# A second buffer for the split queries and keys, and two prepared weights fewer ahead of the first MLP

## The chip, the core and the metric

The kernel runs on one core of a Trainium2 chip. The time is that of the device in microseconds (us) for one execution, and the median of several executions stands for a kernel. The engines of a core are TensorE (PE; the loads of its stationary operand are listed apart as PEld), VectorE (DVE), ScalarE (ACT), GpSimd (POOL) and SyncE (SP), which here issues nearly all DMAs. Each engine takes its instructions strictly in the order in which they were written for it.

## The reference

```python
# B, H, S, D = 4, 8, 576, 64; all float32 (some MLP weights come as float64)
q_rot, k_rot = rotate(q), rotate(k)                       # rotary embedding over D
scores = D ** -0.5 * q_rot @ k_rot.T                      # per batch and head: 576 x 576
attn = softmax(scores)
x = (attn @ v) as [2304 tokens, 512]                      # heads side by side
g = s * relu(x @ w_in) ** 2 + b                           # first MLP: 512 -> 2048
x = g @ w_out                                             # 2048 -> 512
out = (silu(x @ w_gate) * (x @ w_val)) @ w_out2           # second MLP: 512 -> 1536 -> 512
```

## The kernel before

Float32 accuracy is kept by splitting every matmul operand into a high part (rounded to the format that PE multiplies) and a low part (the rest); a product is then two or three matmuls, high by high and the mixed ones.

**Attention** goes over 16 pairs of heads. For each pair, `prep(p)` loads q and k into a tile `x` (two buffers), rotates them on POOL in four steps that end at L495, and transposes them on PE (`pst`, L515) in three groups. From each group ACT writes the high part into the tile `qkhi` (L524) and DVE the low part into `qklo` (L526). Ten DMAs from SP (L548) then copy pieces of `qkhi` and `qklo` to other partitions, into the operand tiles `a`, `t` and `kz`. Of these there are two sets, one for even and one for odd pairs, so the copies of pair p wait until the scores of pair p-2 are done. `pair(p)` computes nine strips of scores (`ps_s`, L620), their maximum on DVE (L623) and exponentials on ACT (L627, tile `e`), transposes those (`ps_t`, L681), splits them into `ph` (ACT, L689) and `pl` (DVE, L696) and multiplies by v (`ps_av`).

`qkhi` and `qklo` have one buffer each. So L524 of pair p, which writes the first group, has to wait until the last copy of pair p-1 has landed.

**First MLP**, in blocks of 512 tokens (later ones 384): for each of 16 chunks f of 128 hidden features, 12 matmuls give `hb` (L810 to L812) from the block's tokens `xh`, `xl` and the split weight "in f"; ACT and DVE make `gh` and `gl` (DVE L872); 12 matmuls with "out f" add to `acc`. PE runs hb of chunk f+2 after acc of chunk f. A weight is loaded as raw float64 (`raw`, three buffers), turned into float32 by one ACT and three DVE instructions (L304, L307, L310, L315, tile `dec`, two buffers), and split by ACT (L342) and by POOL or DVE (L349, tile `w`). The order of the 32 weights is in 0, out 0, in 1, out 1, and so on. The first `WA = 10` of them have memory outside of what attention uses and are prepared while attention runs, the z-th not before a certain strip of scores, their L349 on POOL. The other 22 go into a pool that takes attention's memory when it is free (`switch`, `sw`), so their loads wait for the end of attention, and their L349 is on DVE. The tokens of the first block come from DRAM during attention (`x_load`: loads, a sum and a scaling with `rbx` on POOL at L790 and L793, a split on ACT L797 and DVE L799).

**The order** of all instructions is not written by hand. Each step is given to `Schedule` as an operation with an engine, a duration, a priority (lower goes first), the operations that it needs, and tokens for the buffers that it takes and frees. `Schedule.run` plays this through with its own assumed durations, and whenever an engine is free it emits the ready operation of best priority. The instruction order on every engine is what comes out of this; on the chip each engine keeps that order, whatever the real durations are.

Of the kernel before, what the change touches and what calls it, by code (L numbers as in the profile page):

```python
# [9 lines left out]
F32R = mybir.dt.float32r  # L10
# [167 lines left out]
def tile_attention_moe_moe(  # L178
# [17 lines left out]
    B, H, S, D = q.shape  # L196
# [8 lines left out]
    NU = PC  # L205
    QA = PC // 2
    UBS = (512, 512, 512, 384, 384)
    WA = 10
    WB = 22
    NE = 7  # L210
    LATE, LAST = 1 << 20, 1 << 21
    WARM = 75
    TP = 100
# [8 lines left out]
    sch = Schedule()  # L222
    op = sch.op
    sch.free.update({
        "raw": 3, "dec": 2, "wa": WA, "x": 2, "vr": 2, "ry": 1, "hi": 1, "vh": 3, "opb0": 1, "opb1": 1, "l": 2, "lb": 2, "cr": 1, "e": NE, "ph": 2, "pl": 2,
        "xr": 2, "rbx": 1, "s": 2, "t": 3, "v": 1, "xhb": 1, "gb": 2, "rb2": 3,
    })

# [1 line left out]
    dram = ctx.enter_context(tc.tile_pool(name="dram", bufs=1, space=DRAM))  # L230
    wa_p = ctx.enter_context(tc.tile_pool(name="wa", bufs=WA))
    raw_p = ctx.enter_context(tc.tile_pool(name="raw", bufs=3))
    dec_p = ctx.enter_context(tc.tile_pool(name="dec", bufs=2))
    late = {}
# [11 lines left out]
    att = ExitStack()  # L246
# [2 lines left out]
    vr_p = att.enter_context(tc.tile_pool(name="vr", bufs=2))  # L249
    rp_p = att.enter_context(tc.tile_pool(name="rp", bufs=1))  # L250
    v_p = att.enter_context(tc.tile_pool(name="v", bufs=3))
    ph_p = att.enter_context(tc.tile_pool(name="ph", bufs=2))
    pl_p = att.enter_context(tc.tile_pool(name="pl", bufs=2))
    e_p = att.enter_context(tc.tile_pool(name="e", bufs=NE))
# [169 lines left out]
    def prep(p):  # L424
# [6 lines left out]
        st = {} if p else first_st  # L431
# [30 lines left out]
        for g in range(G):  # L462
            cs = slice(g * PC // G, (g + 1) * PC // G)
            eng = "dve" if p == 0 else "pool"
            e = nc.vector if eng == "dve" else nc.gpsimd
            tt = t_dve if eng == "dve" else t_pool
            wide = [128, PC // G, 2, D // 2]
            def views(a, cs=cs):
                return st["x"].rearrange("p c j (a d) -> p c j a d", a=2)[:, cs, :, a], st["ry"][:, cs, :, a]
            def r0(g=g, e=e, views=views, cs=cs, wide=wide):  # L470
                if g == 0:
                    st["ry"] = rp_p.tile([128, PC, 2, 2, D // 2], F32, tag="ry", name="ry")
                e.tensor_tensor(out=views(0)[1], in0=views(1)[0], in1=rt[:, cs, 1:2].to_broadcast(wide), op=ALU.mult)
            def r1(e=e, views=views, cs=cs, wide=wide):
                e.tensor_tensor(out=views(1)[1], in0=views(0)[0], in1=rt[:, cs, 1:2].to_broadcast(wide), op=ALU.mult)
            def r2(e=e, cs=cs):
                xv = st["x"].rearrange("p c j (a d) -> p c (j a) d", a=2)[:, cs]
                e.tensor_tensor(out=xv, in0=xv, in1=rt[:, cs, 0:1].to_broadcast([128, PC // G, 4, D // 2]), op=ALU.mult)
            def r3(e=e, views=views):
                e.tensor_tensor(out=views(0)[0], in0=views(0)[0], in1=views(0)[1], op=ALU.subtract)  # L480
            def r4(e=e, views=views):
                e.tensor_tensor(out=views(1)[0], in0=views(1)[0], in1=views(1)[1], op=ALU.add)
            o = st.get("rope")
            if o is None and p:
                def y0():
                    st["ry"] = rp_p.tile([128, PC, 2, 2, D // 2], F32, tag="ry", name="ry")
                    nc.gpsimd.tensor_tensor(out=views2(0)[1], in0=views2(1)[0], in1=rt[:, :, 2:3].to_broadcast(whole), op=ALU.mult)
                def y1():
                    nc.gpsimd.tensor_tensor(out=views2(1)[1], in0=views2(0)[0], in1=rt[:, :, 1:2].to_broadcast(whole), op=ALU.mult)
                def y2():  # L490
                    xv = st["x"].rearrange("p c j (a d) -> p c (j a) d", a=2)
                    nc.gpsimd.tensor_tensor(out=xv, in0=xv, in1=rt[:, :, 0:1].to_broadcast([128, PC, 4, D // 2]), op=ALU.mult)
                def y3():
                    xv = st["x"].rearrange("p c j d -> p (c j d)")
                    nc.gpsimd.tensor_tensor(out=xv, in0=xv, in1=st["ry"].rearrange("p c j a d -> p (c j a d)"), op=ALU.add)  # L495
                n2 = PC * D
                for y, fn in enumerate((y0, y1, y2, y3)):
                    o = op("pool", t_pool(n2 if y < 2 else 2 * n2), fn, pr, (o, *lds[0], *rt_op), (ry_tok,) if y == 0 else (), (ry_tok,) if y == 3 else ())
                st["rope"] = o
            elif not p:  # L500
              o = None
              for y, fn in enumerate((r0, r1, r2, r3, r4)):
                deps = [o, *lds[g], rt_op[g]]
                if y == 0 and g > 0:
                    deps.append(st["first"])
                o = op(eng, tt(fd if y == 2 else fd // 2), fn, pr + g, deps, (ry_tok,) if y == 0 and g == 0 else (),
                       (ry_tok,) if y == 4 else (), port=eng == "dve")
                if y == 0 and g == 0:
                    st["first"] = o
            ps_tok = Token("t")  # L510
            def tr(g=g):
                st["ps", g] = ps = ps_t.tile([128, 512], F32, tag="t", name="pst")
                rv = st["x"].rearrange("p c j d -> p c (j d)")
                for c in range(PC // G):
                    nc.tensor.transpose(taken(ps)[:, :, c * 64:(c + 1) * 64], rv[:, g * (PC // G) + c], ident.rearrange("p (h r) -> p h r", h=2))  # L515
            acq = (ps_tok, hi_tok if p > 1 else tok) if g == 0 else (ps_tok,)
            prt = pr + 3 + g
            o = st["tr"] = op("pe", 0.33, tr, prt, (o, eye_op, st.get("tr"), *(zeros[z] if p < 2 else ())), acq, (x_tok,))
            if p > 1:
                def hi(g=g):  # L520
                    if g == 0:
                        st["hi"] = rp_p.tile([128, 2 * S], F32R, tag="hi", name="qkhi")
                        st["lo"] = rp_p.tile([128, 2 * S], F32R, tag="lo", name="qklo")
                    nc.scalar.activation(out=place(st["hi"], g), in_=taken(st["ps", g]), func=AF.Copy, scale=qs_t)  # L524
                def lo(g=g):
                    nc.vector.scalar_tensor_tensor(  # L526
                        out=place(st["lo"], g), in0=taken(st["ps", g]), scalar=qs_t, in1=place(st["hi"], g).bitcast(F32), op0=ALU.mult, op1=ALU.subtract
                    )
                o = st["hi0"] = op("act", t_act(CG, True, 1), hi, prt, (o, qs_op, st.get("hi0")))
                trs.append(op("dve", t_dve(CG, 2), lo, prt, (o,), (), (ps_tok,)))  # L530
            else:
                def act(dst, rows, g=g):
                    scale = D ** -0.5 if rows is up else 1.0
                    return lambda: nc.scalar.activation(out=place(dst, g), in_=taken(st["ps", g])[rows], func=AF.Copy, scale=scale)
                def sub(dst, src, rows, g=g):
                    scale = D ** -0.5 if rows is up else 1.0
                    return lambda: nc.vector.scalar_tensor_tensor(
                        out=place(dst, g), in0=taken(st["ps", g])[rows], scalar=scale, in1=place(src, g).bitcast(F32), op0=ALU.mult, op1=ALU.subtract
                    )
                o1 = op("act", t_act(CG), act(t[dn], dn), prt, (o,))  # L540
                o2 = op("act", t_act(CG), act(a[up], up), prt, (o,))
                ops += [o1, o2, op("dve", t_dve(CG), sub(a[dn], a[up], up), prt, (o2,), (), (ps_tok,))]
                ops.append(op("act", t_act(CG), act(kz[up], dn), prt, (o,), (), (ps_tok,)))
                ops.append(op("dve", t_dve(CG), sub(t[up], t[dn], dn), prt, (o1,), (), (ps_tok,)))
# [373 lines left out]
    n_att = len(sch.ops)  # L918
    for z in range(WA):
        weight(("out" if z % 2 else "in", z // 2), ("wa",), TP * NP, after=s_turns[WU0 + WUS * z:][:1])  # L920
# [8 lines left out]
    def block_b(i, j):  # L929
        st = {}  # L930
        UB = UBS[j]
        prio = LATE + 1000 * i
        pieces, deps, batches = [], [], []
        for o, m, b, s in x_pieces(sum(UBS[:j]), UB, S):
            pieces.append((o, m, (x_d[0][b][:, s:s + m], x_d[1][b][:, s:s + m])))
            batches.append((b, s, m, o))
            deps += x_store[b]
        outs, xh_tok = x_load(st, pieces, UB, prio - 800 if i else LATE - 900, deps, ("xhb", "xhc"), lambda: late[st["xh_tok"].pool], batches, "dve" if i else "pool")
        toks = (Token("s"), Token("s"))

        def get_acc(m):
# [430 lines left out]
```

## Time and profile before

| | |
|---|---|
| time, median of 3 (range) | 1137.23 us (1137.05 to 1138.14) |
| profiled execution: time, span | 1137.79 us, 1136.0 us |
| PE busy, PEld busy | 1106.9 us (97%), 1010.6 us (89%) |
| DVE, ACT, POOL busy | 799.5 us (70%), 591.2 us (52%), 191.0 us (17%) |
| mean granted TensorE clock | 0.991 |

Shares are over the whole span, and its stages differ. Attention lasts until about 317 us and keeps four engines busy; the first MLP's first block follows until about 403 us. After that PE is busy in practically every slice, and the page shows DVE and ACT far from full there. The ends of matmuls are modelled, so short pauses between them don't show as idle time.

### The profile page before, as it was taken

Reading aid. Unit: us, or ns where it says so; the run is one execution under the profiler, and the core shown is the slowest. Engines: PE = TensorE matmul, PEld = TensorE weight load, DVE = VectorE, ACT = ScalarE, POOL = GpSimd, SP = SyncE. Lnnn points to the kernel's source line nnn. Section 1 sums busy time; section 2 is a strip of 40 time slices with the busy share of each in tenths; the row PEclk is TensorE's granted clock in tenths of the full one; section 3 lists DMA queues with packets and bytes.
Section 4 is the critical chain, followed back from the end, with each engine's and each line's share of the span. In section 5 each row is a group of like instructions: output and inputs, shape, how many; then the busy total and the mean of one; then the engine's idle time right before and its main releaser. Section 6 shows DMA issues by size and latency. Waiting matters only on the chain. (4 is left out here: it accounts for less than half of the span.)

```text
span 1136.0 us, 17995 instructions
## 1 busy us (share of the span) xinstructions
PE 1106.9 (97%) x6314; PEld 1010.6 (89%) x6314; DVE 799.5 (70%) x1394; ACT 591.2 (52%) x1199; POOL 191.0 (17%) x156
## 2 busy tenths in 40 slices
PE   8999899999999999999999999999999999999998
PEld 7889888898988888888899999999979999899986
DVE  5889788999979858768768765555565555655560
ACT  4879788889978854444545543322242222422230
POOL 5776776662210000000000000000000000000000
PEclk8899999999999999999999999999999999999999
DMA  5487987877375466575675775766656553575501
GB/s 114 112 200 173 239 206 192 199 169 195 89 230 176 136 199 222 200 242 205 229 237 181 257 251 190 253 193 206 206 177 207 196 193 108 191 224 197 187 10 47
DMA packets 185721, 211.17 MB, mean 186 GB/s; under 512 B 71824, under 2 KB 121120, under 8 KB 185632
## 3 DMA queue, kind: packets, MB, share of 16 engines
q1 hardware_dynamic: 185392, 209.63, 61.8%
q8 instruction: 51, 0.84, 0.3%
q10 hardware_dynamic: 240, 0.39, 0.1%
q14 instruction: 38, 0.31, 0.1%
HBM read 142.07 MB, written 47.26 MB: 167 GB/s over the span
## 5 line engine op out<-in xcount | busy, mean ns | idle before, releaser
L1242 DVE TENSOR_TENSOR tmp<-hb,tmp 128x384 f32<-128x384 f32 x252 | 140.0, 556 | 114.0 <-PE hb L812 113.2
L812 PE MATMUL hb<-xh,w 128*128 128x384 f32 (+1 forms) x560 | 198.9, 355 | 0.0
L810 PE MATMUL hb<-xh,w 128*128 128x384 f32 (+1 forms) x560 | 198.8, 355 | 0.0
L811 PE MATMUL hb<-xl,w 128*128 128x384 f32 (+1 forms) x560 | 198.7, 355 | 0.0
L811 PE MATMUL acc<-gl,w 128*128 128x512 f32 (+1 forms) x320 | 117.8, 368 | 0.1
L810 PE MATMUL acc<-gh,w 128*128 128x512 f32 (+1 forms) x320 | 117.9, 368 | 0.0
L812 PE MATMUL acc<-gh,w 128*128 128x512 f32 (+1 forms) x320 | 117.6, 367 | 0.0
L623 DVE TENSOR_REDUCE nm<-ps_s 128x1 f32<-128x576 f32 x144 | 108.1, 751 | 11.7 <-PE ps_s L620 10.4
L811 PEld LDWEIGHTS hb<-xl,w 128*128 128x128 f32 x560 | 105.1, 188 | 10.5
L810 PEld LDWEIGHTS hb<-xh,w 128*128 128x128 f32 x560 | 105.1, 188 | 10.3
L812 PEld LDWEIGHTS hb<-xh,w 128*128 128x128 f32 x560 | 105.1, 188 | 8.0
L627 ACT ACTIVATE e<-ps_s,nm 128x576 f32<-128x576 f32 x144 | 107.0, 743 | 8.5 <-DVE nm L623 7.8
L620 PE MATMUL ps_s<-t,a 128*128 128x288 f32 x320 | 103.2, 338 | 8.1 <-ACT e L627 6.5
L689 ACT ACTIVATE ph<-ps_t 128x512 fp32r<-128x512 f32 x192 | 105.7, 570 | 9.6 <-PE ps_t L681 7.9
L711 PE MATMUL ps_av<-ph,vh 128*128 128x384 f32 (+1 forms) x320 | 98.0, 327 | 0.8 <-ACT xr L724 0.7
L696 DVE TENSOR_TENSOR pl<-ps_t,ph 128x512 fp32r<-128x512 f32 x144 | 96.0, 682 | 2.3 <-ACT ph L689 1.2
L681 PE MATMUL ps_t<-ident,e 128*128 128x128 f32 x576 | 88.5, 281 | 7.4 <-DVE qklo L526 4.8
L1257 ACT ACTIVATE tmp<-tmp 128x384 f32<-128x384 f32 x72 | 37.8, 524 | 111.2 <-DVE tmp L1242 108.9
L620 PE MATMUL ps_s<-kz,a 128*128 128x288 f32 x320 | 92.4, 304 | 0.1
L811 PE MATMUL hb<-w 128*128 128x384 f32 x264 | 88.9, 337 | 0.0
L812 PE MATMUL hb<-w 128*128 128x384 f32 x264 | 88.8, 337 | 0.0
L810 PE MATMUL hb<-w 128*128 128x384 f32 x264 | 88.5, 335 | 0.0
(118 smaller groups left out, 2304.1 us busy)
## 6 DMA issues: line engine op xcount, KB each, us to landing
w<-wd SPq DMA_DIRECT2D x120, 512.0 KB, 4.3
wd<-w SPq DMA_DIRECT2D x48, 512.0 KB, 3.6
raw<-in_moe_w_out_dram SPq DMA_DIRECT2D x28, 512.0 KB, 3.9
x_d<-xr SPq DMA_DIRECT2D x64, 144.0 KB, 2.5
w<-wd SPq DMA_DIRECT2D x36, 256.0 KB, 3.5
raw<-in_moe_w_in_dram SPq DMA_DIRECT2D x16, 512.0 KB, 3.9
raw<-in_moe_w_gate_dram SPq DMA_DIRECT2D x12, 512.0 KB, 5.2
raw<-in_moe_w_val_dram SPq DMA_DIRECT2D x12, 512.0 KB, 6.6
```

The source lines that it names most:

```text
L620: nc.tensor.matmul(ps[:, hf * 512:hf * 512 + HS], a[:, q0:q0 + 128], m[:, k0:k0 + HS], start=y == 0, stop=y == len(todo) - 1)
L623: nc.vector.tensor_reduce(out=st["nm"][:, u:u + 1], in_=st["s", u], axis=AX.XY, op=ALU.max, negate=True)
L627: nc.scalar.activation(out=st["e", u].rearrange("p (f n) -> p f n", f=2), in_=st["s", u], func=AF.Exp, bias=st["nm"][:, u:u + 1], accum_ou ...
L681: nc.tensor.transpose(ps[:, z * 128:z * 128 + 128], st["e", u][:, kc * 128:kc * 128 + 128], ident)
L689: nc.scalar.activation(out=st["ph", y][0:rows, 512 * i:512 * i + n], in_=st["pt", y, i][0:rows, 0:n], func=AF.Copy)
L696: nc.vector.tensor_tensor(out=dst, in0=st["pt", y, i][0:rows, 0:n], in1=st["ph", y][0:rows, c].bitcast(F32), op=ALU.subtract)
L711: nc.tensor.matmul(ps, vv, st["ph", y][:, c], start=kc == 0, stop=kc == 4)
L810: nc.tensor.matmul(o, lh, rh, start=first, stop=False)
L811: nc.tensor.matmul(o, lh, rl, start=False, stop=False)
L812: nc.tensor.matmul(o, ll, rh, start=False, stop=last)
L1242: nc.vector.tensor_tensor(out=st[dst, f], in0=ps[z], in1=st[a, f], op=ALU.add)
L1257: nc.scalar.activation(out=st[key, f], in_=st[key, f], func=AF.Silu)
```

## The change

`qkhi` and `qklo` get a pool of their own with two buffers each, and the planner's token "hi" allows two. Eight instead of ten weights lie outside of attention's memory: the last two, in 4 and out 4, join the 22 others (24 in all), with L349 on DVE and loads behind the end of attention. The first block's `x_load` gets priority 1200 instead of one behind all of attention; its operations now go ahead of those of the last pairs (pair 12's begin at 1200) wherever both are ready.

```diff
-    WA = 10
-    WB = 22
+    WA = 8
+    WB = 24
...
-        "raw": 3, "dec": 2, "wa": WA, "x": 2, "vr": 2, "ry": 1, "hi": 1, "vh": 3, "opb0": 1, "opb1": 1, "l": 2, "lb": 2, "cr": 1, "e": NE, "ph": 2, "pl": 2,
+        "raw": 3, "dec": 2, "wa": WA, "x": 2, "vr": 2, "ry": 1, "hi": 2, "vh": 3, "opb0": 1, "opb1": 1, "l": 2, "lb": 2, "cr": 1, "e": NE, "ph": 2, "pl": 2,
...
+    hl_p = att.enter_context(tc.tile_pool(name="hl", bufs=2))
...
-                        st["hi"] = rp_p.tile([128, 2 * S], F32R, tag="hi", name="qkhi")
-                        st["lo"] = rp_p.tile([128, 2 * S], F32R, tag="lo", name="qklo")
+                        st["hi"] = hl_p.tile([128, 2 * S], F32R, tag="hi", name="qkhi")
+                        st["lo"] = hl_p.tile([128, 2 * S], F32R, tag="lo", name="qklo")
...
-        outs, xh_tok = x_load(st, pieces, UB, prio - 800 if i else LATE - 900, deps, ("xhb", "xhc"), lambda: late[st["xh_tok"].pool], batches, "dve" if i else "pool")
+        outs, xh_tok = x_load(st, pieces, UB, prio - 800 if i else TP * 12, deps, ("xhb", "xhc"), lambda: late[st["xh_tok"].pool], batches, "dve" if i else "pool")
```

The number of instructions of each kind stays, apart from two L349 that move from POOL to DVE. But the planner starts from other conditions, so the order changes on every engine. Line numbers behind 251 are greater by one in the changed kernel; the text keeps those of before. Three places show the order.

On ACT, the place where `prep(7)` writes its high parts (pairs count from 0; `e` are the exponentials of strips, `ph` the high parts of transposed ones, `pst` the transposed queries and keys). Before:

```order
L689 ACTIVATE ph_1689<-ps_t_1707 128x512
L627 ACTIVATE e_1745,l_1374<-ps_s_1716,nm_1640 128x576
L724 ACTIVATE xr_1661<-ps_av_1673 128x384
L689 ACTIVATE ph_1689<-ps_t_1748 64x384
L524 ACTIVATE qkhi_1777<-pst_1767,qs_203 128x2x192
L524 ACTIVATE qkhi_1777<-pst_1773,qs_203 128x2x192
L627 ACTIVATE e_1798,l_1374<-ps_s_1754,nm_1640 128x576
```

And with the change:

```order
L690 ACTIVATE ph_1545<-ps_t_1531 128x512
L628 ACTIVATE e_1549,l_1396<-ps_s_1508,nm_1395 128x576
L690 ACTIVATE ph_1545<-ps_t_1552 128x512
L628 ACTIVATE e_1567,l_1396<-ps_s_1539,nm_1395 128x576
L525 ACTIVATE qkhi_1579<-pst_1569,qs_206 128x2x192
L525 ACTIVATE qkhi_1579<-pst_1575,qs_206 128x2x192
L628 ACTIVATE e_1598,l_1396<-ps_s_1562,nm_1395 128x576
```

Before, 49 exponentials stand ahead of it (pair 5 is at its fourth strip), now 42 (pair 4, sixth strip): it has moved ahead by seven of a pair's nine strips. On PE its transposes stood behind 5.6 pairs' score matmuls and now stand behind 4.8; for pair 4 it is 2.8 and 2.4, for pair 5 it is 3.6 and 3.0, and from pair 7 to pair 15 the move is 0.6 to 0.8 pairs.

On DVE in the first block, the place where the weight "in 11" is finished (`w_5181` before, `w_5239` now) among the low parts `gl` of chunks. Before, with `gl_5172` that of chunk 9:

```order
L310 SCALAR_TENSOR_TENSOR dec_5165<-raw_5099,dec_5165 128x512
L349 TENSOR_TENSOR w_5181<-dec_5138,w_5181 128x512
L315 SCALAR_TENSOR_TENSOR dec_5165<-raw_5099,dec_5165 128x512
L793 TENSOR_TENSOR xs_5131<-xs_5131,rbx_5153 128x256
L307 TENSOR_SCALAR dec_5194<-dec_5194 128x512
L310 SCALAR_TENSOR_TENSOR dec_5194<-raw_5145,dec_5194 128x512
L872 TENSOR_TENSOR gl_5172<-r_5173,gh_5171 128x512
```

With the change, where `gl_5217` is that of chunk 10:

```order
L316 SCALAR_TENSOR_TENSOR dec_5199<-raw_5139,dec_5199 128x512
L311 SCALAR_TENSOR_TENSOR dec_5209<-raw_5160,dec_5209 128x512
L794 TENSOR_TENSOR xs_5211<-xs_5211,rbx_5169 128x256
L873 TENSOR_TENSOR gl_5217<-r_5218,gh_5216 128x512
L350 TENSOR_TENSOR w_5239<-dec_5199,w_5239 128x512
```

The weight came ahead of chunk 9's `gl` and now comes directly behind chunk 10's.

On PE at the same chunk, the step from acc of chunk 9 to hb of chunk 11. Before (`w_5084` is "out 9"):

```order
L810 MATMUL acc_4737<-gh_5171,w_5084 128x512
L811 MATMUL acc_4737<-gl_5172,w_5084 128x512
L812 MATMUL acc_4737<-gh_5171,w_5084 128x512
L810 MATMUL hb_5254<-xh_1723,w_5181 128x512
L811 MATMUL hb_5254<-xl_1724,w_5181 128x512
```

With the change (`w_5133` is "out 9", `w_5190` is "out 10"):

```order
L813 MATMUL acc_4733<-gh_5156,w_5133 128x512
L811 MATMUL acc_4732<-gh_5216,w_5190 128x512
L812 MATMUL acc_4732<-gl_5217,w_5190 128x512
L813 MATMUL acc_4732<-gh_5216,w_5190 128x512
L811 MATMUL hb_5252<-xh_1774,w_5239 128x512
L812 MATMUL hb_5252<-xl_1775,w_5239 128x512
```

The first three matmuls of chunk 10's acc, which need chunk 10's `gl`, now stand ahead of hb of chunk 11; in the other chunks the alternation is as before. At the seam, the first three hb matmuls of the first block now stand ahead of the last nine of attention's `ps_av`, where before hb began behind all of them.

## Rows read from the trace of the kernel before

**Rows 1.** Windows: start:end, length, busy us of PE, PEld, DVE, ACT, POOL, clock, ...

```profile
40.00:317.00 277.00, 262.28 (x1983) 245.74 (x1982) 250.21 (x402) 242.00 (x571) 164.28 (x129) 0.99 0.74 180
285.00:315.00 30.00, 29.41 (x224) 27.21 (x222) 29.62 (x51) 28.84 (x67) 7.00 (x8) 1.00 0.30 76
323.00:403.00 80.00, 79.92 (x351) 65.41 (x350) 67.39 (x120) 64.61 (x108) 0.00 (x0) 1.00 0.57 176
140.00:145.00 5.00, 4.73 (x26) 4.63 (x27) 4.15 (x8) 3.84 (x10) 1.99 (x3) 0.66 0.90 204
```

**Rows 2.** Timeline of PE, attention: start, duration, instruction, idle before and releaser.

```profile
72.56 0.40 PE L620 MATMUL ps_s<-t,a 128*128 128x288 f32 x1 [2.61 <-ACT e L627]
...
87.01 1.18 PE L681 MATMUL ps_t<-ident,e 128*128 128x128 f32 x8 [0.69 <-DVE qklo L526]
...
140.27 1.97 PE L681 MATMUL ps_t<-ident,e 128*128 128x128 f32 x8 [2.88 <-DVE qklo L526]
...
197.11 0.66 PE L681 MATMUL ps_t<-ident,e 128*128 128x128 f32 x4 [1.24 <-DVE qklo L526]
```

**Rows 3.** Timeline of ACT, attention: the writes of `qkhi`.

```profile
71.20 0.58 ACT L524 ACTIVATE qkhi<-pst,qs 128x384 fp32r<-128x384 f32 x1 [2.67 <-DMA x_d<-xr]
...
138.98 1.05 ACT L524 ACTIVATE qkhi<-pst,qs 128x384 fp32r<-128x384 f32 x2 [4.24 <-DMA kz<-qkhi]
```

**Rows 4.** Line L524: what its engine waited for before it (us, times).

```profile
  DMA kz<-qkhi: 8.0, 4
  DMA x_d<-xr: 5.7, 3
```

**Rows 5.** Issue of a pair's last copy (timeline of SP), and landing times of L548.

```profile
136.07 0.59 SPq L548 DMA_DIRECT2D kz<-qkhi  x1
...
DMA to landing us min/median/max: 2.4/3.0/4.9
```

**Rows 6.** Timeline of ACT: first exponential of pairs 1, 4, 5 and 15.

```profile
40.48 0.72 ACT L627 ACTIVATE e<-ps_s,nm 128x576 f32<-128x576 f32 x1
...
95.24 0.74 ACT L627 ACTIVATE e<-ps_s,nm 128x576 f32<-128x576 f32 x1
...
112.22 0.76 ACT L627 ACTIVATE e<-ps_s,nm 128x576 f32<-128x576 f32 x1
...
295.64 0.73 ACT L627 ACTIVATE e<-ps_s,nm 128x576 f32<-128x576 f32 x1
```

**Rows 7.** Groups of DVE, 100 to 317 us: shapes, count, busy, mean ns, idle before.

```profile
L310 DVE SCALAR_TENSOR_TENSOR dec<-raw,dec 128x512 uint32<-128x512 uint32 x10 | 8.8, 890 | 0.0
...
L307 DVE TENSOR_SCALAR dec<-dec 128x512 uint32<-128x512 uint32 x10 | 5.4, 538 | 0.0
```

**Rows 8.** Groups of DVE, 323 to 403 us (first block).

```profile
L310 DVE SCALAR_TENSOR_TENSOR dec<-raw,dec 128x512 uint32<-128x512 uint32 x22 | 15.2, 690 | 0.5
...
L349 DVE TENSOR_TENSOR w<-dec,w 128x512 fp32r<-128x512 f32 x22 | 15.1, 686 | 2.7 <-ACT w L342 2.7
```

**Rows 9.** Timeline of DVE, first block: "in 11" and "in 15" finished.

```profile
368.48 0.68 DVE L349 TENSOR_TENSOR w<-dec,w 128x512 fp32r<-128x512 f32 x1
...
394.14 0.68 DVE L349 TENSOR_TENSOR w<-dec,w 128x512 fp32r<-128x512 f32 x1
```

**Rows 10.** Timeline of PE, first block: hb of chunks 11 and 15 begin.

```profile
374.69 0.39 PE L810 MATMUL hb<-xh,w 128*128 128x512 f32 x1
...
396.90 0.39 PE L810 MATMUL hb<-xh,w 128*128 128x512 f32 x1
```

**Rows 11.** Timeline of POOL: last step of the rotation of pairs 4 and 7.

```profile
57.74 2.66 POOL L495 TENSOR_TENSOR x<-x,ry 128x1152 f32<-128x1152 f32 x1
...
97.23 2.66 POOL L495 TENSOR_TENSOR x<-x,ry 128x1152 f32<-128x1152 f32 x1
```

**Rows 12.** Timeline of PE: first transposes of pairs 4 and 7.

```profile
67.74 0.49 PE L515 MATMUL pst<-ident,x 128*128 128x128 f32 x3
...
118.34 0.82 PE L515 MATMUL pst<-ident,x 128*128 128x128 f32 x6
```

## The prediction

> **What bounds the kernel now.** I began with the page, whose shares stand in the table above: PE is busy nearly throughout, so a gain has to come from the stage where it is not. The windows say where [rows 1]. In attention, from 40 to 317 us, PE is busy for 262.3 of 277 us, but DVE for 250.2 and ACT for 242.0: three engines are within 13% of full, and a wait on one quickly becomes a wait on the others. Towards the end (285 to 315 us) DVE is full, 29.6 of 30 us. In the first MLP block PE is full, 79.9 of 80 us, and DVE has 12.6 us over. Behind it nothing that the change touches can hold PE up: the order there is of the same shape.
>
> The timeline of PE shows what interrupts attention [rows 2]. Four of its pauses, 2.61, 0.69, 2.88 and 1.24 us, together 7.42 us, end when ACT's exponential or DVE's `qklo` is done. The timeline of ACT has the cause of the first and third a moment earlier [rows 3]: L524, the write of `qkhi`, stood waiting for a DMA for 2.67 and 4.24 us, and DVE and PE ran dry behind it. Over the run ACT lost 8.0 and 5.7 us to this, seven times [rows 4]. The label of three of these names a store from `xr`, but SP's times decide: the last copy out of `qkhi` was issued at 136.07 us and a copy lands 3.0 us later in the median, 139.1; L524 starts at 138.98 [rows 3, 5]. So it is the single buffer: pair p must not write before pair p-1's copies have left.
>
> **The change part by part. The second buffer.** With two, L524 of pair p waits for the copies of pair p-2, a pair earlier, and these have landed. What it wins is at least bounded by what PE shows: 7.42 us of pauses [rows 2], and the clock that the longest one costs. In the 5 us behind it the granted clock is 0.66 of full on average [rows 1], so 68% of them, 3.4 us, ran at 1.2 GHz in place of 2.4; that did the work of 1.7 us, a loss of 1.7. Together 9.1 us. The upper bound is another row: from pair 1 to pair 15 the first exponentials are 255.2 us apart, 14 pairs; pair 4, in which PE and ACT show no wait for a copy, took 16.98 us [rows 6]. At that pace 14 pairs take 237.7, 17.4 us less. The lower bound is 0: another wait may take the place. I take 9.1, since these are pauses seen, and other pairs also hold work that pair 4 lacks (weights, the first block's tokens).
>
> **What is late next.** The transposes of a pair need its rotation on POOL. They now stand 0.4 pairs earlier for pair 4, some 7 us at 17 us a pair. The rotation ended at 60.40 and the transposes began at 67.74 [rows 11, 12]: 7.3 us of slack, all but used. For pair 7 the slack is 118.34 - 99.89 = 18.5 us and the move 0.8 pairs, 13.6 us. The rotations too can move up, because transposing earlier frees `x` earlier, but POOL must first get its loads. I charge 1 us for the early pairs, with bounds of 0 and of what the rival below makes of it.
>
> **Two weights out of attention.** They leave three DVE instructions each. At L310's contended 0.89 us twice (L315 has its shape) and L307's 0.54 [rows 7] that is 2.3 us each, 4.6 for both, and it is an upper bound. They were the last two, in the stretch where DVE is full, so most of it counts: I take 3, lower bound 0 (if ACT's exponentials or PE set the pace there). L310 is longer here than in the first block, 0.89 against 0.69 us [rows 7, 8], while POOL works beside it. The Trainium skill's page "SBUF — State Buffer", section "SBUF: two separate sides", says more: a DVE instruction with two SBUF inputs and a GpSimd one that reads SBUF exclude each other for a whole instruction. By that rule four such instructions could each have stood behind a 2.66 us rotation step [rows 11], 10.6 us, and the sum would end near 1120; the mean of ten shows 0.2 us each, so I don't use it.
>
> **The same two in the first block.** DVE gets four instructions each, three at 0.69 and the shift, not above 0.54 [rows 7, 8]: 2.6 us each, 5.2 together, into 12.6 us of room [rows 1]. That alone would cost nothing. But weights come just in time: "in 11" was ready at 369.16 and used at 374.69, 5.5 us to spare; "in 15" at 394.82 and 396.90, only 2.1 us [rows 9, 10]. Each "in f" now takes about the place that "in f+1" had. From "in 11" to "in 15" eight weights were finished in 25.7 us, 3.2 us each; two more at this pace come 6.4 us later, minus 2.1 us to spare: a loss of 4.3 us, my upper bound. The lower one is 0, if DVE draws on its room. In the order the weight "in 11" has slipped behind chunk 10's `gl`, and PE has been given three matmuls of acc ahead of hb 11 which need that `gl`; a pause there is likely. I take 2 us.
>
> **The tokens of the first block.** L799's two last instructions used to stand at the seam and now come before it, and hb can begin among the last `ps_av`. I count it as nothing: hidden by PE's own last attention matmuls; without that cover it moves by two DVE instructions, 1.4 us at the 0.69 of [rows 8].
>
> **Sum.** Against the profiled execution of 1137.79 us (span 1136.0): -9.1 + 1 - 3 + 2 = -9.1, so 1128.7. That execution lies 0.6 us above the median shown, so I say 1128.
>
> **The rivals.** *Larger:* attention runs all pairs at pair 4's pace. The first term is then 17.4 in place of 9.1, and the time 1120. For it: ACT's own waits sum to 13.7 us [rows 4], more than PE's pauses, and the pauses between matmuls are partly hidden in modelled ends. The Trainium skill's page "Perfetto Trace Analysis", section "Identifying the Most-Contended Engine", holds LDWEIGHTS busy time for the better measure of room on TensorE; by the row for it there are 31.3 us free in attention, not 14.7 [rows 1]. Against it: the later pairs have DVE full.
>
> *Smaller:* the rotation, SP's loads or the planner's tighter order bring back half of the 9.1, and the first block loses the full 4.3. Then -4.5 + 1 - 3 + 4.3 = -2.2: 1135. One half of this is enough for 1132.
>
> *Slower:* the rotation becomes the stall. PE keeps its order, so if a transpose waits for L495, all matmuls behind it wait. With thirteen pairs moved up (3 to 15), 0.7 us each eats the 9.1; at 1.5 us each the term is +19.5, and the time about 1147. For it speaks pair 4, with nothing to spare; against it pair 7, with 4.9 us left even if its rotation did not move at all.
>
> That the second buffer is not used is ruled out by the order on ACT: L524 stands seven strips earlier.
>
> **How the numbers follow.** The forecast (1124 to 1132) gets 0.50, the larger gain (1116 to 1124) 0.18, the smaller (1132 to 1137) 0.20, the slower (above 1137) 0.12. 1118 to 1136 leaves out the slow case and edges of the larger and smaller one, less than 2 in 10. A measurement of this kernel tells some 0.2%, 2.3 us, from no change: below 1134.9 is faster. That takes in the first two cases and most of the third, 0.84; the same gets 0.06; slower 0.10.
>
> **What the profile will show.** If I am right: L524 no longer waits for a DMA; the pauses of PE before L681 and L620 with `qklo` or an exponential as releaser are gone or under 1 us; hb of the first block begins some 10 to 12 us earlier than 317 us; the clock stays full between 60 and 317 us; from there to the end of the first block it takes 1 to 4 us longer, with PE waiting near chunk 10's `gl` or a weight; and the rest is as long as before. I am wrong if PE's transposes wait for L495, if SP's copies now hold up score matmuls, or if the first block loses more than attention gives.

## The result, and the profile after

The changed kernel takes 1143.39 us, median of six runs (1140.45 to 1148.23), where before takes 1137.14 beside it: a ratio of 1.0054, 95% interval 1.0034 to 1.0074. It is slower by some 6 us, and its runs lie 8 us apart where those of before lie 2. (That is little to tell a scatter from: with 15 to 34 executions on one chip, beside the experiments below, those of before lie 4 to 9 us apart.) The execution in the profile is the slowest of the six, so a second one (e1 below, 1140.74 us) is read beside it.

The windows of the changed kernel, columns as in [rows 1], show a good start and two bad stretches.

```profile
40.00:124.00 84.00, 83.80 (x659) 80.64 (x658) 78.29 (x127) 77.63 (x183) 59.05 (x42) 1.00 0.78 187
124.00:200.00 76.00, 64.26 (x469) 61.00 (x468) 59.82 (x94) 57.14 (x135) 50.30 (x41) 0.91 0.82 207
200.00:260.00 60.00, 52.09 (x384) 49.66 (x383) 54.69 (x80) 47.64 (x112) 36.06 (x29) 0.94 0.66 161
```

Up to 124 us PE is busy throughout (83.80 of 84 us) and pair 6 begins 4.5 us earlier than before (first exponential at 124.14 against 128.67). In the next 76 us PE lacks 11.7 us, in the 60 behind that 7.9, and the granted clock falls to 0.91 and 0.94. The timeline of PE has the two pauses, which answer to [rows 2] (lines are one higher from L252 on):

```profile
143.25 1.12 PE L682 MATMUL ps_t<-ident,e 128*128 128x128 f32 x4 [7.45 <-DVE qklo L527]
224.27 0.61 PE L621 MATMUL ps_s<-t,a 128*128 128x288 f32 x1 [5.93 <-ACT e L628]
```

**The first pause** is the old one, larger. The timeline of ACT, beside [rows 3]:

```profile
141.97 1.05 ACT L525 ACTIVATE qkhi<-pst,qs 128x384 fp32r<-128x384 f32 x2 [7.80 <-DMA x_d<-xr]
```

As before, the label names a store, and SP's times decide. This is the write of pair 9's `qkhi`, which reuses the buffer of pair 7, and the copies of pair 7 left SP only now. The timeline of SP:

```profile
100.36 0.54 SPq L661 DMA_DIRECT2D r_d<-rr  x1
105.65 0.66 SPq L447 DMA_DIRECT2D vr<-in_v_dram  x1
...
118.86 1.08 SPq L763 DMA_DIRECT2D xl<-x_d  x1
120.05 0.44 SPq L763 DMA_DIRECT2D xh<-x_d  x1
120.58 1.58 SPq L733 DMA_DIRECT2D x_d<-xr  x2
122.21 0.65 SPq L447 DMA_DIRECT2D vr<-in_v_dram  x1
122.90 0.64 SPq L445 DMA_DIRECT2D vr<-in_v_dram  x1
123.59 0.65 SPq L447 DMA_DIRECT2D vr<-in_v_dram  x1
124.29 0.97 SPq L445 DMA_DIRECT2D vr<-in_v_dram  x1
125.88 0.60 SPq L449 DMA_DIRECT2D vr<-in_v_dram  x1
128.91 1.75 SPq L779 DMA_DIRECT2D rbx<-r_d  x2
130.76 0.58 SPq L393 DMA_DIRECT2D x<-in_q_dram  x1
131.38 0.72 SPq L393 DMA_DIRECT2D x<-in_k_dram  x1
132.15 1.05 SPq L549 DMA_DIRECT2D a<-qkhi  x1
...
138.71 0.59 SPq L549 DMA_DIRECT2D kz<-qkhi  x1
```

The last copy is issued at 138.71, and 3 us later ACT goes on. The buffers that these copies fill were free when the last score matmul of pair 5 ended, at 120.3 us, and `qkhi` and `qklo` of pair 7 had long been written. The ten copies began at 132.15, 11.9 us later (4.5 in the kernel before), behind eleven other transfers. Two waits of SP are part of it, one long before and one among these transfers. The view of SP's waits, 90 to 135 us, names both:

```profile
SPq L447 <- POOL vh L571: 5.1, 1, 5.1
SPq L779 <- DMA xh<-x_d: 2.4, 1, 2.4
```

At 100.9 SP stood 5.1 us at a load into `vr`, that of pair 6, until POOL had done with the tile of pair 4. POOL's last `vh` of that tile (L573) ran behind steps of a rotation (L493, L496) that had been moved up: it is that of pair 8, which ends at 104.79 here and at 118.81 in the kernel before. The timeline of POOL, and then the same `vh` in the kernel before:

```profile
99.06 2.67 POOL L493 TENSOR_TENSOR x<-x,rt 128x1152 f32<-128x1152 f32 x1
101.69 0.46 POOL L571 TENSOR_SCALAR vh<-vr 128x320 fp32r<-128x320 f32 x1
102.12 2.67 POOL L496 TENSOR_TENSOR x<-x,ry 128x1152 f32<-128x1152 f32 x1
104.75 0.87 POOL L573 TENSOR_TENSOR vh<-vr,vh 128x320 fp32r<-128x320 f32 x1
```

```profile
100.41 0.87 POOL L572 TENSOR_TENSOR vh<-vr,vh 128x320 fp32r<-128x320 f32 x1
```

At 126.5 SP stood 2.4 us until a transfer of 1024 KB, `xh`, had landed. So ACT came to its `qkhi` no later than in [rows 3] (141.97 - 7.80 = 134.2, against 138.98 - 4.24 = 134.7), while the copies were released 3.0 us later (141.97 against 138.98): 4.24 + 0.57 + 2.99 = 7.80.

**The second pause** begins on DVE. The timelines of DVE and POOL:

```profile
214.24 0.68 DVE L697 TENSOR_TENSOR pl<-ps_t,ph 128x512 fp32r<-128x512 f32 x1
214.84 7.25 DVE L800 TENSOR_TENSOR xl<-xs,xh 128x512 fp32r<-128x512 f32 x1
222.01 0.68 DVE L311 SCALAR_TENSOR_TENSOR dec<-raw,dec 128x512 uint32<-128x512 uint32 x1
```

```profile
213.68 1.42 POOL L490 TENSOR_TENSOR ry<-x,rt 128x576 f32<-128x576 f32 x1
215.06 0.46 POOL L571 TENSOR_SCALAR vh<-vr 128x320 fp32r<-128x320 f32 x1
215.48 2.67 POOL L493 TENSOR_TENSOR x<-x,rt 128x1152 f32<-128x1152 f32 x1
218.10 0.87 POOL L573 TENSOR_TENSOR vh<-vr,vh 128x320 fp32r<-128x320 f32 x1
218.92 2.62 POOL L496 TENSOR_TENSOR x<-x,ry 128x1152 f32<-128x1152 f32 x1
```

L800, which writes the low part of the tokens, takes 0.55 to 0.84 us elsewhere in this trace. Here it took 7.25: it began while POOL's L490 was running and ended just behind the next four POOL instructions, which followed each other without a gap (215.06 to 221.54). The change's new priority had moved it from the end of attention into pair 10.

### The profile page after: what moved, and what is told of

It is laid out like the page before. It is cut to its first block, busy times and chain, and to the rows that moved or that the text cites. A ratio compares the mean times of both kernels' runs of the same rounds, so it can differ in the third digit from the quotient of the medians.

```text
span 1146.4 us, 18013 instructions
## 1 busy us (share of the span) xinstructions
PE 1108.6 (97%) x6314; PEld 1014.1 (88%) x6314; DVE 807.3 (70%) x1396; ACT 593.3 (52%) x1199; POOL 186.6 (16%) x154
## 5 line engine op out<-in xcount | busy, mean ns | idle before, releaser
L712 PE MATMUL ps_av<-ph,vh 128*128 128x384 f32 (+1 forms) x320 | 100.9, 337 | 0.5 <-ACT xr L725 0.4
```

Of the source, the lines that this page charges most:

```text
L712: nc.tensor.matmul(ps, vv, st["ph", y][:, c], start=kc == 0, stop=kc == 4)
```

## The experiments

Where nothing else is said, a ratio is to the kernel before on the same chip, with its 95% interval. All are built on the kernels of this case; "buffers" are the change's two `qkhi`/`qklo` buffers and eight weights.

**e1: the change once more.** No edit.

> The changed kernel once more, for a second profile. Run-ahead theory: the copies of pair 7 are again issued late by SP, and ACT's qkhi of pair 9 waits 6 to 8 us for them, near the first exponential of pair 7; this stall belongs to the order and is there in every execution. Lock theory: DVE's L800 of the first block's tokens is again far longer than its usual 0.7 us, where POOL has the rotation beside it; the length may differ, since it hangs on how the two engines happen to meet (1 to 8 us). Rival (the first block pays): neither stall is needed, and the block is 4 us or more longer than 86.5. Time 1140 to 1148.

1140.74 us, a single execution. The first pause is there again (ACT's L525 waits 7.56 us, SP's waits are 5.0 and 2.0), so it belongs to the order. The second is not:

```profile
214.78 1.18 DVE L800 TENSOR_TENSOR xl<-xs,xh 128x512 fp32r<-128x512 f32 x1
```

```profile
215.38 0.90 POOL L571 TENSOR_SCALAR vh<-vr 128x320 fp32r<-128x320 f32 x1
216.25 3.10 POOL L493 TENSOR_TENSOR x<-x,rt 128x1152 f32<-128x1152 f32 x1
```

With the same neighbours, DVE got in between POOL's instructions: L800 took 1.18 us, and this time POOL's L571 and L493 took 0.4 us longer each. The two executions differ by 7.5 us in time, and by 7.9 in the end of attention; at the first exponential of pair 10 they are 0.1 us apart (208.51 and 208.41), at that of pair 11, behind the second pause, 8.4.

**e2: buffers only.** The planner is told of one buffer where there are two, and the tokens keep their old priority, so that the second buffer can only be slack.

```
-        ... "hi": 2, ...
+        ... "hi": 1, ...
-        outs, xh_tok = x_load(..., prio - 800 if i else TP * 12, ...)
+        outs, xh_tok = x_load(..., prio - 800 if i else LATE - 900, ...)
```

> The buffers of the change (two for qkhi and qklo, eight weights) with the planner still told of one, and the first block's tokens loaded at their old priority: the order in attention is that of before but for the two weights. Run-ahead theory: now the second buffer is slack and nothing else; L524's waits of 2.67 and 4.24 us vanish, and the sum of the prediction holds without its charge for earlier transposes, 1137.8 - 9.1 - 3 + 2 = 1127.7, so 1126 to 1131. Lock theory alone: L800 back at its place, faster than the change by 6 to 8 us. Rival (the first block or the memory pays): 1137 or more.

0.9992 (0.9979 to 1.0005): no difference from before (1137.9 us, where I had expected 1126 to 1131). The mechanism of the prediction is there: no `qkhi` waits for a copy any more, and at pair 7 attention is 8.6 us ahead (first exponential at 141.25 against 149.89). Then ACT meets the next late transfer, the first weight's load:

```profile
157.34 0.66 ACT L305 ACTIVATE dec<-raw 128x512 f32<-128x512 f32 x1 [8.63 <-DMA raw<-in_moe_w_in_dram]
```

```profile
131.46 0.59 SPq L549 DMA_DIRECT2D t<-qkhi  x1
...
152.09 0.59 SPq L292 DMA_DIRECT2D raw<-in_moe_w_in_dram  x1
```

Between these two rows of SP stand 28 other issues, nearly without a gap: 29 in 20.6 us, 0.71 us each. Before issued the same load at 155.06. ACT was 8.6 us ahead, SP only 3.0.

**e3: the change with the old token priority.**

```
-        outs, xh_tok = x_load(..., prio - 800 if i else TP * 12, ...)
+        outs, xh_tok = x_load(..., prio - 800 if i else LATE - 900, ...)
```

> The change but for one line: the first block's tokens at their old priority, so that L800's instructions leave the middle of attention. Lock theory as the whole cause: the 7.25 us instruction and what followed it (5.9 us of PE and the clock behind it) are gone, and with nothing else wrong the time comes to some 1130. Run-ahead theory: the stall at pair 7 (7.45 us of PE and its clock) stays, since qkhi is still planned ahead; 1143.4 - 6 to 8 gives 1135 to 1138. Rival (first block): 1143, no better than the change.

1.0028 (1.0013 to 1.0043): still slower than before. Its 1141.7 us is above the 1135 to 1138 of the run-ahead theory and below the 1143 of the rival. ACT's L525 waits 7.87 us and SP 4.8 at `vr`; three of the four L800 are back at the end of attention.

**e4: the weights only.** Before, with `WA, WB = 8, 24`.

> The kernel before with eight weights in attention instead of ten, and nothing else of the change. By the prediction's terms -3 + 2 = -1, so 1136; its bounds are 1132.5 (-4.6) and 1141.5 (+4.3). Rival (the two weights are what makes the change slow): 1141 to 1143. Run-ahead and lock theories both: 1134 to 1138, since neither stall has to do with the weights.

1.0010 (0.9996 to 1.0024): not told from before. Its 1139.9 us, beside 1138.4 for before, lies between the 1134 to 1138 of the two theories and the 1141 to 1143 of the rival. Against e2 it shows the second buffer as slack alone: 1.0010 to 0.9992, some 2 us, at the edge of the intervals.

**e5, e6, e7: seven copies for ten.** In before (e5), in buffers only (e6) and in the change (e7) the pairs of copies into `t` and `kz` are one issue each; the planner still counts ten, so that the order stays.

```
-                c = slice(s0, s0 + S)
-                ops.append(sp(t[64:128, c], lambda c=c: st["hi"][64:128, c]))
...
+                c = slice(0, 2 * S) if s0 == 0 else None
+                ops.append(sp(t[64:128, c or slice(s0, s0 + S)], c and (lambda c=c: st["hi"][64:128, c])))
...
```

The two other copies of this loop are changed likewise; in its second pass (`s0` is `S`) the planner's operation stays and issues nothing.

> The kernel before, with seven copies out of qkhi and qklo a pair in place of ten: each of the three pairs of copies into t and kz is one issue of 288 KB instead of two of 144, same bytes, same order on PE, DVE, ACT and POOL. Theory of the full queue (SP issues 26 to 28 transfers in 20 us, back to back, in pairs 4 to 10, and what waits for it is only a sign): every pair saves SP 3 x 0.64 = 1.9 us, and the waits of 2.67, 1.93, 4.24 and 2.13 us for copies shrink by that or more; 3 to 6 us faster, 1132 to 1135 where before takes 1138. Rival (the DMA engines, 0.8 busy, are what is full): same bytes, so no change, 1137 to 1139. Rival (the single buffer itself): a copy lands as late or later in the larger piece, no change or 1 us slower.

> The kernel of buffers only (two of qkhi and qklo, planned as one) with the merged copies. Theory of the full queue: SP reaches the weight's load at pair 8 two to three pairs' savings earlier, 4 to 6 us, so ACT's wait of 8.63 us for it shrinks to 3 to 5, and the time to 1131 to 1134; it gains as much from the merging as the kernel before or more. Rival (DMA engines full): no change from buffers only, 1137 to 1139. If the second buffer is worth something of its own once SP has room, this is 2 us or more below the kernel before with merged copies; if not, the two are equal.

> The change with the merged copies. Theory of the full queue: ACT's wait of 7.8 us for pair 7's copies shrinks by 1.9 to 4, and the time by 3 to 6, to 1137 to 1140. The long L800 may come or not, as in the change. Rival (DMA engines full): 1141 to 1144.

e5: 0.9984 (0.9970 to 0.9998). e6: 0.9963 (0.9950 to 0.9977), ACT's wait for the first weight 5.55 us where it was 8.63. e7: 1.0019 (1.0004 to 1.0034), with a wait of 8.79 us for pair 7's copies, not less: SP stood 5.5 us at `vr` and 3.4 for `xh`. So fewer issues help, with the same bytes, but by 2 to 4 us, less than the 3 to 6 that the full queue was to give: 1137.2 us in e5, 1135.3 in e6 and 1141.4 in e7 are all outside of its ranges, and e7's wait went the other way. In e5 23 issues keep SP busy for 17.0 us (60 to 80 us) where 27 took 18.0 before, so an issue is not a fixed 0.64 us; what makes some longer is not shown. e6 lies 1.8 us below e5, so the second buffer as slack is again worth some 2 us.

**e8: the true issue cost.** The change, with 0.65 us an issue in the planner instead of 0.55.

```
-        o = self.op(eng, 0.55, fn, prio, deps, acq, rel)
+        o = self.op(eng, 0.65, fn, prio, deps, acq, rel)
...
```

> The change, with the planner told 0.65 us for an issue on SP, as the trace shows, in place of 0.55: a new order on every engine. Theory of the full queue: the plan no longer puts ACT's qkhi and the weights' first instruction ahead of what SP can deliver, so the wait of 7.8 us at pair 7 falls under 3 us, and the time to 1132 to 1137. Rival (the order's detail decides, and no single cost): some other wait of 5 us or more comes up, 1139 or more.

0.9998 (0.9983 to 1.0013). The wait at pair 7 is gone and SP stands only 0.5 us at `vr`; the longest pause of PE is 3.02 us. This one number, which changes the order on every engine, takes back what the change lost, and no more: 1138.1 us lies above the 1132 to 1137 of the theory, without the long wait that the rival asks for.

**e9, e10, e12: later weights.** The planner reckons a weight's load as landing 8 us later, in e2's kernel (e9), in e6's (e10), and in e10's with the tokens loaded in four pieces (e12).

```
-                        o.done = dma_free + 1.3
+                        o.done = dma_free + 1.3 + o.lag
...
+        o.lag = 8.0 if after else 0.0
```

> The kernel of buffers only, with the planner told that each of the eight weights lands 8 us later than it thought, so that ACT's first instruction of a weight (L305) stands further behind its load; nothing else. Theory (ACT's in-order queue meets whichever transfer is late on SP, and its wait of 8.63 us for the first weight is a matter of where L305 was put): that wait falls under 2 us, the lead of 8.6 us that attention had at pair 7 is kept, and the time is 1129 to 1133 where before takes 1138 to 1139. Rival (SP or the transfers are full, so the time comes back wherever the order lets it): another wait of 5 us or more, 1136 to 1139.

> The same with the merged copies, that is, buffers only, seven copies a pair and weights planned as landing 8 us later. Both theories of the queue add: the 5.55 us wait that was left with merged copies is gone as well, and the time 1127 to 1132; below the kernel with merged copies alone (1135.3) by 3 us or more. Rival (transfers full): 1134 to 1137, no better than merged copies alone.

> The kernel with merged copies and later weights, and the first block's tokens loaded as four transfers of 512 KB in place of two of 1024. In every trace so far SP stands 2.0 to 3.4 us, eight transfers behind the second of these, until it has landed. If it is their length that holds SP: this wait is gone, at the price of two issues (1.3 us), and the time 1 to 2 us below the unsplit kernel, or equal. Rival (SP waits because the engines that carry the data are full): the wait stays, in one place or another, and the time is equal or 1 us more.

1.0459, 1.0414 and 1.0437: the edit also hit the weights of `w_out2` in the second MLP, whose loads are planned by the same function, and behind the first block these kernels take 43 to 47 us longer. Their times say nothing of attention, so only its trace is used. In e9 the 8.63 us wait is gone and three others are there, 4.11, 3.63 and 4.41 us on PE, and the first hb begins at 313.84, later than e2's 311.93. In e10 the 5.55 us wait is gone too, pauses of 3.00 and 3.87 us are there, and the first hb begins at 309.56 (e6: 308.97). In these two profiles, moving the instruction that waits wins nothing. In e12 SP still stands 1.7 us in two pieces where it stood 3.2 in e10; what that is worth stays open.

**e11: the priority only.** The change, planned with one buffer: `"hi": 1`.

> The buffers of the change, planned as one, but with the first block's tokens at the change's new priority: against the kernel of buffers only this is the priority alone, against the change the planning with two buffers alone. If the two edits add: 0.0026 above buffers only (ratio 1.002, some 1141), since taking the priority out of the change won 0.0026. Theory of the lock (an early L800 meets the rotation on POOL): a DVE instruction of 2 us or more among L800 in attention, in some executions, and a wider scatter. Rival (the priority is harmless by itself): 1138, as buffers only.

0.9988 (0.9974 to 1.0001). This is one token of the planner away from the change, with the same buffers, and 0.0066 lower. With e2 and e3 it completes a square (ratios to before):

| | old token priority | new token priority |
|---|---|---|
| two buffers, planned as one | 0.9992 (e2) | 0.9988 (e11) |
| two buffers, planned as two | 1.0028 (e3) | 1.0054 (the change) |

The priority by itself costs nothing; planning with two buffers costs 0.0036 with the old priority and 0.0066 with the new one. (Each ratio is good to 0.0013 to 0.0020, so these two are not told apart.) The long L800 that the lock theory asked for is there, 2.41 and 2.05 us, but the time is that of its rival.

**e13: a plan that knows SP.** The change; the planner takes 0.65 us for an issue, and starts none before the transfer eight back has landed.

```
-                while busy.get(eng, 0.0) <= now + 1e-9 and ready[eng]:
+                while busy.get(eng, 0.0) <= now + 1e-9 and ready[eng] and not (eng == "sp" and len(flight) >= 8 and flight[-8] > now + 1e-9):
...
+                            flight += [o.done] * max(1, round(o.dur / 0.65))
...
```

> The change, planned with SP as the trace shows it: 0.65 us an issue, and no issue before the transfer eight back has landed. Theory of the wrong picture: the copies of pair 7 no longer stand behind nine others, and no wait of 5 us or more is left on PE; 1131 to 1136 where before takes 1138 to 1139, and below the run with the true issue cost alone (0.9998). Theory that SP has no more to give: equal to that run, 1136 to 1140.

0.9971 (0.9952 to 0.9990), 1135.5 us: as the theory of the wrong picture said, a little faster than before, with both buffers planned. Its interval still meets that of e8. No pause of PE is over 2.1 us, and the copies of pair 7 begin 0.3 us after their buffers are free. Its windows:

```profile
40.00:124.00 84.00, 80.50 (x618) 77.10 (x617) 74.99 (x116) 73.10 (x171) 62.00 (x43) 0.98 0.77 179
124.00:200.00 76.00, 74.09 (x566) 69.55 (x566) 70.06 (x113) 68.56 (x162) 50.59 (x42) 1.00 0.87 222
```

It is slower than the change up to 124 us (80.50 us of PE against 83.80) and then keeps going: 74.09 of 76 us where the change had 64.26, at full clock. From pair 5 to 8 the first exponentials are 16.5 us apart.

**e14, e15: the same planner, seven copies planned,** with two buffers (e14) and one (e15).

> The same planner and two buffers, with seven copies a pair (t and kz in one issue each, planned so). Theory of the wrong picture: SP has room now and the plan knows it; both gains add, 1127 to 1133. Theory that SP or the transfers have no more to give: 1133 to 1137, as the buffers only with merged copies (1135.3).

> The same as the last with the second buffer there but planned as one, so that it is only slack on the chip. If a second buffer is worth something once the picture is right, this is 2 us or more above the last; if running ahead has no worth by itself, equal; if run-ahead is the harm whatever the planner knows of SP, 3 us or more below it.

1.0025 (1.0007 to 1.0044) and 1.0032 (1.0013 to 1.0051): 1141.4 us is a miss for both theories of e14. e15 equals it: by its expectation, running ahead has no worth by itself here, and it is not the harm either. In e14 SP stands 4.7 us at a `vr` load again, and ACT's `qkhi` waits 6.17 us; in e15 ACT waits 6.43 us for the first weight. So knowing the queue does not keep the planner from such an order.

**e16, e17, e18: the fastest.** The copies merged in the code alone, in e11's kernel (e16), in e13's (e17) and in e13's planned with one buffer (e18).

> The change with its two buffers planned as one (0.9988 of before) and the copies merged in the code alone, so that the order stays. Merging took 0.0016 off the kernel before, 0.0029 off buffers only and some 0.0035 off the change: 0.996 of before here, 1134 to 1135; the fastest so far if the edits add.

> The change planned with SP as the trace shows it (0.9971 of before), and the copies merged in the code alone, so that the order stays. Merging in the code alone took 0.0016 to 0.0035 off four kernels: 0.994 to 0.9955 here, 1131.5 to 1133. If the corrected plan already keeps every copy ahead of its reader, fewer issues win nothing: 0.997.

> The same with the two buffers planned as one. If planning with two buffers is worth something once the picture of SP is right, this is slower than the run before it by 0.002 or more; if the corrected plan alone is the gain, the two are equal within 0.002; if running ahead is the harm whatever the planner knows, this is the faster by 0.002 or more.

0.9956 (0.9939 to 0.9973), 0.9950 (0.9934 to 0.9966) and 0.9968 (0.9956 to 0.9981). e16 and e17 take 1133.8 and 1134.1 us where before takes 1138.4 and 1139.2 beside them, and beat both kernels of this case; by their ratios both are as expected, and e18 is equal to e17 within the 0.002 set for it. In five kernels now, merging the copies in the code took 0.0016 to 0.0035. Two buffers against one, with the corrected plan, differ by 0.0018, within the intervals: whether planning with two is worth anything is not settled.

## Why the prediction was wrong

It said 1128 us and 1118 to 1136; the time is 1143.4. By the end of PE's last `ps_av` matmul each profiled execution splits into attention and the rest (its span less that end):

| | attention ends | the rest |
|---|---|---|
| before | 317.4 | 818.6 |
| e4, eight weights | 317.5 | 820.1 |
| e2, and a second buffer as slack | 314.4 | 820.0 |
| e1, the change | 318.6 | 820.3 |
| the change, profiled run | 326.5 | 819.9 |
| e13, plan that knows SP | 311.9 | 821.8 |

**The step that failed** is the sentence "With two, L524 of pair p waits for the copies of pair p-2, a pair earlier, and these have landed." The planner spends the second buffer: it writes `qkhi` 0.77 of a pair earlier in the plan (pair 9's at 6.67 pairs, where before wrote pair 8's at 6.44 and pair 9's at 7.44), so the copies it waits for are again those made a moment ago. I had read this shift in the order and used it as proof that the buffer is used; it was also the proof that the slack is gone. The transposes, rotations and loads that move with it set POOL and SP a task they could not meet, and SP's 5 us at `vr` came out of that. All five profiles with a stand of 4.7 to 5.5 us there (the change, e1, e3, e7, e14) have a `qkhi` wait of 6.2 to 8.8 us that ends between 140 and 145 us; no other has one over 5.0. In these five, and in no other, POOL has the rotation of pair 8 ahead of pair 4's last `vh`. The other stand, for `xh`, does not go with the wait: e14 has none of it, and e8 and e13 have 2.4 and 2.5 us of it while no `qkhi` waits for a copy. That the stand at `vr` is the cause, and not only its companion, rests on SP's order and on e8 and e13, in which it is 0.5 and 1.7 us; it was not taken away by itself, and a stand alone does not make the wait (e16 has one of 4.6 us at another `vr` load, with slack in the buffers, and no `qkhi` waits there).

**The term of -9.1** failed even where the slack was real. e2 has no wait for a copy and was 8.6 us ahead at pair 7, and won 3.1 us of attention (317.5 to 314.4). (The sum of pauses was also incomplete: one of 1.98 us before L515 at 216.12, with `qklo` as releaser, is not in it.) I had named three engines within 13% of full and left out a fourth, SP. It was in the same trace of before: between 60 and 200 us it issues 24 to 28 transfers in every 20 us, and is busy for 15.4 to 18.2 of them. The single buffer's wait was the place where a late queue became visible. The bound of 0 that I gave this term, "another wait may take the place", is what came.

**The two weights.** Out of attention they win nothing (317.4 to 317.5; I took 3, with 0 as the bound). In the first block they cost 1.3 to 1.7 us by the rest (I took 2): about right; behind that block, before, e4, e2 and e1 all take 729.3 to 729.4 us. These are single profiles, and e5, with the weights and the order of before, has a rest of 819.0.

**The transposes' slack** (I charged 1): no stall by a rotation on PE in the change, so the slower rival's mechanism, PE waiting for L495, was wrong though its sign was right. The rotation did its harm on POOL's own queue, ahead of `vh`.

**The tokens**, counted as nothing, are the second pause. I had weighed the Trainium skill's page "SBUF — State Buffer", section "SBUF: two separate sides", and set its exclusive lock aside because ten instructions showed 0.2 us each in the mean. The section says that whichever instruction starts first holds the shared pair to its end and the other blocks. The L800 of 7.25 us beside POOL agrees with that and is worse, since it began during L490 and DVE got in at none of the four boundaries that followed; the L800 of 1.18 us in e1 shows the same meeting with another outcome. A mean of 0.2 us did not rule out such a single case. That the lock makes the change's runs scatter by 8 us fits these two executions but is not shown: the four runs in between have no profile, before scatters about as much over more executions, and in e11 an L800 of 2 us and more cost nothing.

Adding up for e1: +0.1 (weights in attention) - 3.1 (slack) + 4.2 (planned run-ahead) + 1.7 (the rest) = +2.9, from 1137.79 to 1140.74; the long L800 adds 7.5 in the other execution. The 4.2 is what is left between e2 and e1 (314.4 and 318.6), so the tokens' new priority is in it as well.

The *smaller* rival had the right word, "SP's loads or the planner's tighter order", and half the size. Of what I said the profile would show, the early part came (up to pair 6 no `qkhi` waits for a copy and PE is busy throughout), and not the rest: hb began at 323.96 (316.04 in e1) instead of 305 to 307.

## What to carry to other kernels

Here the wait for a buffer showed where a late queue was met first. Before a buffer is added, look at the queue that releases it: count its issues in a stretch of 20 us, and ask which in-order engine meets the next late transfer and at what distance. And where a planner sets the order, a second buffer told to the planner can be spent on running ahead; given on the chip alone, it is slack (worth some 2 us here). If such a plan loses, its picture of the queue (cost of an issue, transfers in flight) is worth correcting before its resources are: here that took the same buffers from 1.0054 to 0.9971. It is no guarantee: the same corrected planner with seven copies planned gave 1.0025.

## What the runs showed of the hardware

- SP's issues go eight deep here. In the rows above SP stands at L779, the eighth transfer behind the 1024 KB load of `xh` (two stores, five loads of `vr`, then `rbx`). In e13 (lines five higher than in the kernel before) the eighth behind it is a copy, which waits 2.5 us for it:

```profile
123.16 0.50 SPq L767 DMA_DIRECT2D xh<-x_d  x1
123.71 1.20 SPq L783 DMA_DIRECT2D rbx<-r_d  x2
125.12 0.63 SPq L451 DMA_DIRECT2D vr<-in_v_dram  x1
125.79 0.62 SPq L449 DMA_DIRECT2D vr<-in_v_dram  x1
126.45 0.61 SPq L451 DMA_DIRECT2D vr<-in_v_dram  x1
127.11 0.62 SPq L449 DMA_DIRECT2D vr<-in_v_dram  x1
128.06 0.52 SPq L553 DMA_DIRECT2D a<-qkhi  x1
131.16 0.52 SPq L553 DMA_DIRECT2D a<-qklo  x1
```

  One long transfer thus holds up whatever the order puts eight places behind it. The records of the traces tell where the eight comes from: SP's issues signal eight semaphores in turn, and the issue that stands waits for the one that it is to signal itself, number 106 at L779, which is that of `xh`'s load. So this limit is the program's; whether the chip has one of its own is not shown.
- One DVE instruction, usually of 0.68 us, took 7.25 beside POOL, over four of its instructions, in one execution and 1.18 in the next.
- A kernel's order alone, with the same buffers and the same work, moved the time between 0.9971 and 1.0054 of before.
